# A fused attention and two-MLP kernel: at the passage to the last matrix, landed weight tiles are split before other landed tiles, and the second pass's weights are split five steps later

## The chip, the cores and the metric

The kernel runs on one core of one Trainium2 chip. The core has engines that run side by side, each through its own instructions in program order: TensorE (PE in the rows, its weight loads PEld), VectorE (DVE), ScalarE (ACT), GpSimd (POOL) and SyncE (SP), which here issues every DMA. The metric is device time in microseconds (us), the median over runs of the whole kernel.

## The reference

An attention over 4 x 8 heads of 576 positions (a local part and a part on averaged positions) gives x of 2304 x 512. Two MLPs follow, all in float32:

```python
h = x @ w_in                      # 512 -> 2048
x = (h - tanh(h)) @ w_out         # 2048 -> 512
gate = sigmoid(x @ w_gate)        # 512 -> 1536
val = x @ w_val                   # 512 -> 1536
out = (gate * val) @ w_out2       # 1536 -> 512, the last matrix
```

## The kernel before

**Split operands.** A float32 operand of a large matmul is split into a high part (a rounded copy, made by ACT: "hi") and a low part (operand minus high part, made by DVE: "lo"). One product then is three matmuls in a row on TensorE, `mm3`: L292 (weight high x data high), L293 (weight high x data low) and L294 (weight low x data high). So L292 needs both hi, L293 needs the lo of the data, L294 the lo of the weight.

**The second MLP** is computed in a seven-product scheme for 2 x 2 blocks, so each matrix is stored as seven sums and differences of its blocks (forms). The gate and val stage runs j = 0 to 5 (six pieces of 256 of the 1536 columns), p = 0 to 2 (three pairs of 384-token chunks) and side 0, 1 (gate, val). Its result, gate * val, is made by DVE (L1030), GpSimd forms the sums of it (L1003, in `u_sums`), and SP stores the seven forms of 128 x 384 each to DRAM (names `u_0`, `u_1`, `u_2` for p = 0, 1, 2).

**The last matrix** runs six passes over (p, e): (0,0), (0,1), (1,1), (1,0), (2,0), (2,1); e is one half of the 512 output columns. A pass has six steps i = 0 to 5, a step has seven products in the order `order_b` (forms 0, 4, 3, 5, 1, 2, 6), so a pass is 42 products or 126 matmuls. A weight tile (e, i) holds the seven forms of one step, 128 x 896; (0,0) to (0,5) serve the first pass, (1,0) to (1,5) the second. A data tile (i, form) is one form of step i for one p. The DRAM loads of weight tiles are `w_fetch` (L1057), their hi and lo `w_hi` (L302, through `copy`) and `w_lo` (L1065); of data tiles `u_fetch` (L1080), `u_hi` (L302) and `u_lo` (L1086). In the rows a tile bears the name of the memory that it lies in: weight tiles are `o` or `f` of 128x896, data tiles `x`, `f` or `u` of 128x384 or several of these together. The eight `u` tiles are the last to come in the first pass: form 6 of step 4, and then forms 0 to 6 of step 5.

**What sets the order of the work.** The order on every engine is written out by the program. A counter `now` advances by `tick()`; `defer(n, fn)` puts work n ticks later; "lanes" are generators that are served within ticks under a budget. At the passage from the gate and val stage to the last matrix three lanes run: `first_w` and `first_u` issue the loads as memory comes free, and `first_splits` issues their splits. It takes what was fetched at least six ticks ago, whether the bytes are there or not; the engine that gets the split waits for the bytes:

```python
ready = [x for x in ready if now[0] >= x[0] + 6]
_, kind, x = min(ready)
```

The key of `min` is (tick of the fetch, "u" or "w", tile), so of tiles fetched in one tick the data tiles come first. In the first pass, at the end of step i < 4, the program fetches the second pass's weight tile (1, i+2) 10 ticks later and splits it 10 ticks (hi) and 12 ticks (lo) after that. A step is four ticks. At the end of a pass the seven PSUM banks are read out by ACT (one copy) and DVE (adds, L983), in `out_ends`; later products that use a bank again wait for these.

Of the kernel before, what the change touches and what calls it, by code (L numbers as in the profile page):

```python
# [64 lines left out]
def tile_kernel(ctx: ExitStack, tc: tile.TileContext, qk, vp, v, w1, w2, mask, ident, out):  # L65
# [52 lines left out]
    def defer(n, fn, *args):  # L118
        events.setdefault(now[0] + n, []).append((fn, args))
# [28 lines left out]
    def tick():  # L148
        now[0] += 1
        run_chains(chains.pop(now[0], []))  # L150
        todo = events.get(now[0], [])
        while todo:
            fn, args = todo.pop(0)
            fn(*args)
        events.pop(now[0], None)
        run_later(age=8)
        if beat[0]:
            beat[0]()
        lanes_step()
# [27 lines left out]
    def after(n):  # L187
        at = now[0] + n
        return lambda: now[0] >= at


    loaded, begun, ready, load_at = [0], [0], [0], {}
# [98 lines left out]
    def mm3(o, wh, wl, xh, xl, first, last, **kw):  # L291
        nc.tensor.matmul(out=o, lhsT=wh, rhs=xh, start=first, stop=False, **kw)  # L292
        nc.tensor.matmul(out=o, lhsT=wh, rhs=xl, start=False, stop=False, **kw)  # L293
        nc.tensor.matmul(out=o, lhsT=wl, rhs=xh, start=False, stop=last, **kw)  # L294
# [464 lines left out]
    while any(((1, 0), k) not in xt for k in range(KD)):  # L759
        keep_warm(2)  # L760
        if started[0] < n_first:
            x = items[started[0]]
# [296 lines left out]
    def w_hi(key):  # L1059
        t = w_room[key]  # L1060
        copy(t[:, 0], t[:, 1].bitcast(F32))
# [6 lines left out]
    def pieces(i):  # L1068

        n, todo, at = 7 * i, 7, 0  # L1070
        for g in list(groups):
            size = g[0].shape[1]
            if n < size and todo:
                k = min(size - n, todo)
                yield at, [x[:, n:n + k, :] for x in g]
                at, todo, n = at + k, todo - k, size
            n -= size

    def u_fetch(p, i, at, t):
        nc.sync.dma_start(out=t[1].bitcast(F32), in_=ud[p][:, i, at:at + t[1].shape[1], :])  # L1080

    def u_hi(t):
        copy(t[0], t[1].bitcast(F32))
# [79 lines left out]
    def first_splits():  # L1163

        p = 0
        done = set()
        while len(u_forms) < 7 * NJ or len(fetched_w) < 8 or any(("w", x) not in done for x in fetched_w):
            ready = [(t, "u", x) for x, t in fetched_u.items() if ("u", x) not in done]
            ready += [(t, "w", x) for x, t in fetched_w.items() if ("w", x) not in done]
            ready = [x for x in ready if now[0] >= x[0] + 6]  # L1170
            if not ready:
                yield after(1)
                continue
            _, kind, x = min(ready)
            done.add((kind, x))
            if kind == "w":
                w_hi(x)
                defer(2, w_lo, x)
                yield 1.05
            else:  # L1180
                whole = dict(pieces(x[0]))[x[1]]
                size = whole[0].shape[1]
                for a in range(0, size, 3):
                    t = [y[:, a:min(a + 3, size), :] for y in whole]
                    u_hi(t)
                    defer(2, u_lo, p, x[0], x[1] + a, t)
                    yield 0.1 + 0.45 * t[0].shape[1]

    for j in range(NJ):
        for p in range(len(PAIRS)):  # L1190
            cycle[:] = now[0], p
            for side in range(2):
                while (j, side) not in form or p not in formed:
                    rate[0] = 0.9
                    tick()
                rate[0] = (0.6 if side else 0.9) if j == NJ - 1 else 0.4 if side else 0.65
                w = form[j, side]
                ends = ends_of(j, side, p)
                bank = next(ends)
                if (j, p, side) == (NJ - 1, 0, 0):  # L1200
                    for g in (first_w(), first_u(), first_splits()):
                        lane(g)
                for n, (a, b, at) in enumerate(PRODUCTS):
                    for k in range(2):
                        x = xform[p, k, b]
                        wh, wl = (w[:, i, a, 128 * k:128 * k + 128] for i in range(2))
                        mm3(
                            bank[at], wh, wl, x[:, 0, :], x[:, 1, :], n < 4 and k == 0,
                            k == 1, skip_group_check=n > 3,
                        )  # L1210
                    defer(1, next(ends))
                    tick()
                if p == len(PAIRS) - 1:
                    made.add((j, side))
                made.add((j, side, p))
# [5 lines left out]
    def sum_bank():  # L1221
        n_bank[0] += 1
        k = (n_bank[0] - 1) % 8
        if k < 4:
            return ps.tile([128, 512], F32, tag="ab", bufs=4, name="ab")
        return acc_bank((3, 0, 1, 2)[k - 4])

    def out_ends(q, banks):

        p, e = passes[q]  # L1230
        m1, m6, m5, m7, m2, m3, m4 = (t[:, :N] for t in banks)
        c11, c22, c12, c21 = (xs.tile([128, N], F32, tag="xs", name="c") for _ in range(4))
        to = out[p, e]

        def put(r, half, t, cols=slice(0, N)):
            store(to[:, r, half * N + cols.start:half * N + cols.stop], t[:, cols])

        yield copy(c11, m1)
        yield add(c22, m6, c11)
        yield add(c12, m5, c22)  # L1240
        yield (add(c21, m7, c22), add(c22, m5, c21), defer(1, put, 1, 1, c22))
        yield (add(c11, m2, c11), defer(1, put, 0, 0, c11))
        yield (add(c12, m3, c12), defer(1, put, 0, 1, c12))
        if q < len(passes) - 1:
            yield (add(c21, m4, c21), defer(1, put, 1, 0, c21))
            return
        for cols in (slice(0, N // 2), slice(N // 2, N)):
            add(c21[:, cols], m4[:, cols], c21[:, cols])
            put(1, 0, c21, cols)
        yield None  # L1250

    rate[0] = 0.9
    for q, (p, e) in enumerate(passes):
        ends = None
        for i in range(NJ if q < len(passes) - 1 else NJ - 1):
            both = (i, i + 1) if (q, i) == (len(passes) - 1, NJ - 2) else (i,)
            for m in both:
                while (e, m) not in w_sets or any((p, m, a) not in u_forms for a in range(7)):
                    tick()
            if i == 0:  # L1260
                banks = [sum_bank() for _ in range(7)]
            for n, (a, b) in enumerate(order_b):
                for m in both:
                    x, w = u_forms[p, m, b], w_sets[e, m]
                    mm3(banks[n][:, :N], w[:, 0, a], w[:, 1, a], *x, m == 0, m == NJ - 1)
                if both[-1] == NJ - 1:
                    ends = ends or out_ends(q, banks)
                    defer(1, next, ends)
                if n % 2 or n == 6:
                    tick()  # L1270
            if q + 1 < len(passes) and q % 2 == 0 and i < 4:
                key, wait = (1 - e, (i + 2) % NJ if q == 0 else i), 10 if q == 0 else 1
                defer(wait, w_fetch, key, w_room[e, i])
                defer(wait + 10, w_hi, key)
                defer(wait + 12, w_lo, key)
            if q % 2 and q + 1 < len(passes):
                for k, (at, t) in enumerate(pieces(i)):
                    u_fetch(p + 1, i, at, t)
                    defer(10 + k, u_hi, t)
                    defer(12 + k, u_lo, p + 1, i, at, t)  # L1280
# [70 lines left out]
```

## Time and profile before

| | us |
|---|---|
| median of 3 runs | 923.91 (922.76 to 927.88) |
| the profiled execution: its time | 923.75 |
| the profiled execution: span, first to last instruction | 921.9 |
| TensorE busy | 910.9 (99%) |
| DVE, ACT, POOL busy | 590.1 (64%), 467.1 (51%), 165.1 (18%) |
| first matmul of the last matrix | 785.17 |
| first matmul of its second pass | 808.14 |

The rows below give starts in us from the span's start. A row of a timeline merges neighbours of the same kind: the second number is the time from the first one's start to the last one's end, "x2" the count, and in brackets stands how long the engine sat idle before and what ended that.

### The profile page before, as it was taken

Reading aid. Unit: us, or ns where it says so; the run is one execution under the profiler, and the core shown is the slowest. Engines: PE = TensorE matmul, PEld = TensorE weight load, DVE = VectorE, ACT = ScalarE, POOL = GpSimd, SP = SyncE. Lnnn points to the kernel's source line nnn. Section 1 sums busy time; section 2 is a strip of 40 time slices with the busy share of each in tenths; the row PEclk is TensorE's granted clock in tenths of the full one; section 3 lists DMA queues with packets and bytes.
Section 4 is the critical chain, followed back from the end, with each engine's and each line's share of the span. In section 5 each row is a group of like instructions: output and inputs, shape, how many; then the busy total and the mean of one; then the engine's idle time right before and its main releaser. Section 6 shows DMA issues by size and latency. Waiting matters only on the chain.

```text
span 921.9 us, 16739 instructions
## 1 busy us (share of the span) xinstructions
PE 910.9 (99%) x6392; PEld 876.2 (95%) x6392; DVE 590.1 (64%) x1003; ACT 467.1 (51%) x1166; POOL 165.1 (18%) x185
## 2 busy tenths in 40 slices
PE   7999999999999999999999999999999999999998
PEld 6789989999999999999999999999999999999998
DVE  6799964334343534466875577767767677978582
ACT  5887865444544454443644455353535345655440
POOL 2320102202222020000023243233231314200000
PEclk9999999999999999999999999999999999999999
DMA  8467652222223120457441224343534358987951
GB/s 291 148 233 249 202 156 91 67 62 74 67 66 91 59 78 4 149 217 272 151 141 51 95 95 143 141 168 127 177 115 157 120 161 300 322 294 271 330 203 44
DMA packets 72432, 142.50 MB, mean 155 GB/s; under 512 B 6608, under 2 KB 58400, under 8 KB 68000
## 3 DMA queue, kind: packets, MB, share of 16 engines
q1 hardware_dynamic: 72352, 141.43, 45.3%
q8 instruction: 50, 0.82, 0.4%
q14 instruction: 30, 0.25, 0.1%
HBM read 97.76 MB, written 43.65 MB: 153 GB/s over the span
## 4 chain that ended last, share of the span: by engine, by line
PE 86%; issue 5%; DVE 2%; ACT 2%; DMA 2%; POOL 1%; SPq 0%; POOLq 0%; DVEq 0%
PE ab L292 13%; PE acc L292 13%; PE ab L294 13%; PE ab L293 13%; PE acc L293 13%; PE acc L294 12%; PE ab L539 2%; PE ab L457 1%; PE ab L530 1%; PE acc L755 1%; PE ab L426 1%; PE ab L374 1%; DMA u<-t 1%; PE ab L408 1%; POOL t L1003 1%
## 5 line engine op out<-in xcount | busy, mean ns | idle before, releaser
L305 DVE TENSOR_TENSOR t<-ab,t 128x384 f32<-128x384 f32 x94 | 52.3, 556 | 136.0 <-ACT t L657 135.6
L292 PE MATMUL acc<-g,w 128*128 128x384 f32 x384 | 132.6, 347 | 0.0
L292 PE MATMUL ab<-x,w 128*128 128x384 f32 x376 | 130.8, 348 | 0.1
L293 PE MATMUL acc<-g,w 128*128 128x384 f32 x384 | 129.5, 337 | 0.0
L294 PE MATMUL acc<-g,w 128*128 128x384 f32 x384 | 129.4, 337 | 0.0
L294 PE MATMUL ab<-x,w 128*128 128x384 f32 x376 | 126.5, 336 | 0.0
L293 PE MATMUL ab<-x,w 128*128 128x384 f32 x376 | 126.4, 336 | 0.0
L657 ACT ACTIVATE t<-ab 128x384 f32<-128x384 f32 x94 | 45.9, 488 | 131.0 <-PE ab L294 128.8
L294 PE MATMUL ab<-x,f 128*128 128x384 f32 x261 | 87.8, 336 | 0.8 <-DVE f L1065 0.8
L294 PE MATMUL acc<-x,f 128*128 128x384 f32 x261 | 87.6, 336 | 0.0
L292 PE MATMUL acc<-x,f 128*128 128x384 f32 x261 | 87.6, 336 | 0.0
L293 PE MATMUL acc<-x,f 128*128 128x384 f32 x261 | 87.6, 336 | 0.0
L293 PE MATMUL ab<-x,f 128*128 128x384 f32 x261 | 87.6, 336 | 0.0
L292 PE MATMUL ab<-x,f 128*128 128x384 f32 x261 | 87.6, 336 | 0.0
L305 DVE TENSOR_TENSOR g<-t,g 128x384 fp32r<-128x384 f32 x96 | 56.0, 584 | 39.8 <-ACT g L302 38.5
L292 PEld LDWEIGHTS acc<-g,w 128*128 128x128 f32 x384 | 72.1, 188 | 2.2 <-issue 1.2
L292 PEld LDWEIGHTS ab<-x,w 128*128 128x128 f32 x376 | 70.7, 188 | 3.1 <-issue 1.4
L293 PEld LDWEIGHTS acc<-g,w 128*128 128x128 f32 x384 | 72.3, 188 | 0.4 <-issue 0.2
L294 PEld LDWEIGHTS acc<-g,w 128*128 128x128 f32 x384 | 72.2, 188 | 0.1
L302 ACT ACTIVATE g<-t 128x384 fp32r<-128x384 f32 x96 | 50.0, 522 | 42.1 <-DVE t L305 42.0
L293 PEld LDWEIGHTS ab<-x,w 128*128 128x128 f32 x376 | 70.8, 188 | 0.1
L294 PEld LDWEIGHTS ab<-x,w 128*128 128x128 f32 x376 | 70.7, 188 | 0.1
(186 smaller groups left out, 2018.7 us busy)
## 6 DMA issues: line engine op xcount, KB each, us to landing
raw<-in_w SPq DMA_DIRECT2D x34, 1024.0 KB
u<-t SPq DMA_DIRECT2D x51, 192.0 KB
qk<-in_qk SPq DMA_DIRECT2D x16, 576.0 KB
x<-u SPq DMA_DIRECT2D x9, 960.0 KB
o<-o SPq DMA_DIRECT2D x18, 448.0 KB
u<-c SPq DMA_DIRECT2D x39, 192.0 KB
u<-c SPq DMA_DIRECT2D x18, 384.0 KB
o<-f SPq DMA_DIRECT2D x6, 896.0 KB
```

Of the source, the lines that this page charges most:

```text
L292: nc.tensor.matmul(out=o, lhsT=wh, rhs=xh, start=first, stop=False, **kw)
L293: nc.tensor.matmul(out=o, lhsT=wh, rhs=xl, start=False, stop=False, **kw)
L294: nc.tensor.matmul(out=o, lhsT=wl, rhs=xh, start=False, stop=last, **kw)
L302: nc.scalar.activation(out=dst, in_=src, func=ACTF.Copy)
L305: nc.vector.tensor_tensor(out=dst, in0=a, in1=b, op=ALU.subtract)
L374: nc.tensor.matmul(out=sd[t][o0:o0 + 64, at, :], lhsT=qd[r0:r0 + 64, 40 * j:40 * j + 64], rhs=kd[r0:r0 + 64, :], start=True, stop=True,)
L408: nc.tensor.transpose(out=tb[:, 128 * j:128 * j + 128], in_=pd[:, j, 72 * f:72 * f + 72], identity=id_sb)
L426: nc.tensor.matmul(out=ob[64 * h:64 * h + 64, :], lhsT=vd[:, f, 64 * h:64 * h + 64], rhs=pdt[:, f, h].rearrange("p j k -> p (j k)"), start ...
L457: nc.tensor.matmul(out=bank[o0:o0 + 64, at, :], lhsT=t[r0:r0 + 64, 0, QB * j:QB * j + QB], rhs=t[r0:r0 + 64, 1, w0:w0 + WIN], start=True, ...
L530: nc.tensor.transpose(out=tb[:, j, :], in_=pl[:, 3 * f + j, :], identity=id_sb)
L539: nc.tensor.matmul(out=ob[r0:r0 + 64, QB * x:QB * x + QB], lhsT=vw[0][:, j - n, i, r0:r0 + 64], rhs=pt[:, x, o0:o0 + 64], start=True, stop ...
L657: nc.scalar.activation(out=t, in_=hb[:, :N], func=ACTF.Tanh)
```

## The change

`first_splits` takes weight tiles before data tiles, whatever the tick of their fetch; the lo of such a weight tile is put one tick after its hi, not two; and in the first pass hi and lo of the second pass's weight tiles come 15 and 17 ticks after the fetch, not 10 and 12. The fetches themselves are as before.

```diff
-            _, kind, x = min(ready)
+            _, kind, x = min(ready, key=lambda y: (y[1] != "w", y[0], y[2]))
             done.add((kind, x))
             if kind == "w":
                 w_hi(x)
-                defer(2, w_lo, x)
+                defer(1, w_lo, x)
                 yield 1.05
...
                 key, wait = (1 - e, (i + 2) % NJ if q == 0 else i), 10 if q == 0 else 1
+                gone = 15 if q == 0 else 10
                 defer(wait, w_fetch, key, w_room[e, i])
-                defer(wait + 10, w_hi, key)
-                defer(wait + 12, w_lo, key)
+                defer(wait + gone, w_hi, key)
+                defer(wait + gone + 2, w_lo, key)
```

What this does to the order of instructions is shown at three places. The first is ACT at the end of the first pass, before the change. The `f` 128x896 are the weight tiles (0,4) and (0,5), the `u` the last eight data tiles of the first pass, the first two `o` behind them (1,0) and (1,1), `c<-ab` is the first read-out of the first pass's banks, the next four `o` are (1,2) to (1,5), and the `x` are data tiles of the third pass:

```order
L302 ACTIVATE f<-f 128x896 x2
L302 ACTIVATE u<-u 128x384 x8
L302 ACTIVATE o<-o 128x896 x2
L302 ACTIVATE c<-ab 128x384
L302 ACTIVATE o<-o 128x896 x4
L302 ACTIVATE x<-x 128x5x384
L302 ACTIVATE x<-x 128x2x384
L302 ACTIVATE x<-x 128x3x384
```

And after the change:

```order
L302 ACTIVATE f<-f 128x896 x2
L302 ACTIVATE o<-o 128x896 x2
L302 ACTIVATE u<-u 128x384 x8
L302 ACTIVATE c<-ab 128x384
L302 ACTIVATE o<-o 128x896 x3
L302 ACTIVATE x<-x 128x5x384
L302 ACTIVATE x<-x 128x2x384
L302 ACTIVATE o<-o 128x896
L302 ACTIVATE x<-x 128x3x384
```

The two `o` of the second pass, (1,0) and (1,1), moved in front of the eight `u` of the first pass; (1,5) moved behind seven data tiles of the third pass; (1,2), (1,3) and (1,4) kept their place.

The second place is DVE at the same point, with the lo parts, before the change:

```order
L1065 TENSOR_TENSOR f<-f 128x896 x2
L1086 TENSOR_TENSOR u<-u 128x384 x8
L1065 TENSOR_TENSOR o<-o 128x896 x2
L983 TENSOR_TENSOR c<-ab,c 128x384 x4
L983 TENSOR_TENSOR c<-acc,c 128x384 x3
L1065 TENSOR_TENSOR o<-o 128x896 x4
```

And after it:

```order
L1065 TENSOR_TENSOR f<-f 128x896 x2
L1065 TENSOR_TENSOR o<-o 128x896 x2
L1086 TENSOR_TENSOR u<-u 128x384 x8
L983 TENSOR_TENSOR c<-ab,c 128x384 x4
L983 TENSOR_TENSOR c<-acc,c 128x384 x3
L1065 TENSOR_TENSOR o<-o 128x896 x3
```

Here too the lo parts of (1,0) and (1,1) moved in front of those of the eight `u`, and the read-out of the banks (L983) now follows the `u` and no longer the `o`.

The third place is DVE some 15 us earlier, around the last two products gate * val (L1030, the second of which GpSimd's last sums need), before the change. The `o` here are the weight tiles (0,2) and (0,3):

```order
L983 TENSOR_TENSOR c<-acc,three 128x384
L1086 TENSOR_TENSOR x<-x 128x2x384
L1030 TENSOR_TENSOR c<-c 128x768
L983 TENSOR_TENSOR c<-acc,three 128x384
L1086 TENSOR_TENSOR x<-x 128x384
L1030 TENSOR_TENSOR c<-c 128x768
L1086 TENSOR_TENSOR x<-x 128x2x384
L1065 TENSOR_TENSOR o<-o 128x896 x2
```

And after it:

```order
L983 TENSOR_TENSOR c<-acc,three 128x384
L1086 TENSOR_TENSOR x<-x 128x384
L1030 TENSOR_TENSOR c<-c 128x768
L983 TENSOR_TENSOR c<-acc,three 128x384
L1086 TENSOR_TENSOR x<-x 128x3x384
L1030 TENSOR_TENSOR c<-c 128x768
L1086 TENSOR_TENSOR x<-x 128x2x384
L1086 TENSOR_TENSOR x<-x 128x384
```

The `o` of (0,2) and (0,3) moved some ten instructions forward, in front of all these rows, so each data tile here stands later, and between the two L1030 there is now one of three tiles where there was one of one. On TensorE nothing moved; on SP the fetch of (1,5) moved in front of the fourth store of the first pass's output.

## Rows read from the trace of the kernel before

**Rows 1.** The page: span, and busy time of each engine.
```profile
span 921.9 us, 16739 instructions
...
PE 910.9 (99%) x6392; PEld 876.2 (95%) x6392; DVE 590.1 (64%) x1003; ACT 467.1 (51%) x1166; POOL 165.1 (18%) x185
```

**Rows 2.** Windows, the first three passes: length, busy per engine (count), clock, DMA.
```profile
785.17:808.14 22.97, 22.15 (x127) 21.83 (x127) 22.30 (x28) 15.12 (x23) 6.27 (x4) 1.00 0.94 325
808.14:830.50 22.36, 22.03 (x126) 21.50 (x126) 15.67 (x20) 11.32 (x12) 0.00 (x0) 1.00 0.83 289
830.50:852.70 22.20, 22.20 (x130) 22.20 (x129) 18.49 (x27) 13.05 (x19) 0.00 (x0) 1.00 0.78 269
```

**Rows 3.** Waits of TensorE from 600 us on: total, times, longest.
```profile
PE ab L294 <- DVE f L1065: 0.8, 1, 0.8
PE ab L292 <- DVE c L983: 0.3, 1, 0.3
```

**Rows 4.** Timeline of TensorE, end of the first pass, start of the second.
```profile
799.90 0.34 PE L293 MATMUL ab<-x,f 128*128 128x384 f32 x1
801.05 0.44 PE L294 MATMUL ab<-x,f 128*128 128x384 f32 x1 [0.82 <-DVE f L1065]
...
803.93 0.33 PE L292 MATMUL acc<-u,f 128*128 128x384 f32 x1
...
805.15 0.34 PE L293 MATMUL ab<-u,f 128*128 128x384 f32 x1
...
809.58 0.34 PE L294 MATMUL ab<-x,o 128*128 128x384 f32 x1
810.25 0.44 PE L292 MATMUL ab<-x,o 128*128 128x384 f32 x1 [0.33 <-DVE c L983]
```

**Rows 5.** Timeline of ACT, the same stretch and the second pass.
```profile
801.45 1.99 ACT L302 ACTIVATE u<-u 128x384 fp32r<-128x384 f32 x4 [0.46 <-DMA u<-u]
...
805.37 0.95 ACT L302 ACTIVATE o<-o 128x896 fp32r<-128x896 f32 x1 [0.61 <-DMA o<-o]
806.52 0.96 ACT L302 ACTIVATE o<-o 128x896 fp32r<-128x896 f32 x1 [0.19 <-DMA o<-o]
...
820.74 3.81 ACT L302 ACTIVATE x<-x 128x1920 fp32r<-128x1920 f32 x3 [1.65 <-DMA x<-u]
```

**Rows 6.** Timeline of DVE, last gate products to second pass.
```profile
787.83 1.13 DVE L1086 TENSOR_TENSOR x<-x 128x384 fp32r<-128x384 f32 x1
788.89 0.94 DVE L1030 TENSOR_TENSOR c<-c 128x768 f32<-128x768 f32 x1
...
790.62 3.73 DVE L1065 TENSOR_TENSOR o<-o 128x896 fp32r<-128x896 f32 x2
...
801.92 3.83 DVE L1086 TENSOR_TENSOR u<-u 128x384 fp32r<-128x384 f32 x8
806.36 2.24 DVE L1065 TENSOR_TENSOR o<-o 128x896 fp32r<-128x896 f32 x2 [0.61 <-ACT o L302]
808.52 2.27 DVE L983 TENSOR_TENSOR c<-ab,c 128x384 f32<-128x384 f32 x4
...
822.58 6.19 DVE L1086 TENSOR_TENSOR x<-x 128x1920 fp32r<-128x1920 f32 x4 [2.36 <-ACT x L302]
```

**Rows 7.** Timeline of POOL, sums of the last product gate * val.
```profile
787.53 1.02 POOL L1003 TENSOR_TENSOR t<-c 128x384 f32<-128x384 f32 x1 [9.05 <-DVE c L1030]
...
793.49 1.75 POOL L1003 TENSOR_TENSOR c<-c,t 128x384 f32<-128x384 f32 x1
```

**Rows 8.** Timeline of SP: last store of sums, first fetches of the next weights.
```profile
795.26 0.32 SPq L309 DMA_DIRECT2D u<-c  x1
...
799.71 3.02 SPq L1057 DMA_DIRECT2D o<-o  x5
```

**Rows 9.** Line 755 on TensorE, 0 to 9 us and 12 to 20 us: ns min/median/max.
```profile
L755 PE MATMUL acc<-id_sb x10: 421/421/581, 4.8 to 8.8; 128*128 128x128 f32 x10
...
L755 PE MATMUL acc<-id_sb x42: 275/275/377, 12.2 to 19.7; 128*128 128x128 f32 x42
```

## The prediction

> **What bounds the kernel now.** I read the page first: TensorE is busy 910.9 of 921.9 us, the next engine, DVE, 64% [rows 1]. So any time that TensorE is made to wait is added to the span, and a saving on another engine is worth only the wait that it takes away. The next view is therefore the list of TensorE's waits in the part that the change touches. There are two, of 0.8 and 0.3 us [rows 3]. The timeline gives their full cost as the gap between starts, less the 0.17 us at which matmuls follow each other (22.20 us for 126 to 130 of them in an undisturbed pass [rows 2]). The first is 801.05 - 799.90 - 0.17 = 0.98 us: L294 of tile (0,4) waits for DVE's lo of that weight tile. The second is 810.25 - 809.58 - 0.17 = 0.50 us: the fourth product of the second pass waits for a bank that DVE has yet to read out [rows 4]. Together 1.5 us; the third pass shows none [rows 2]. More than 1.5 us can hardly be won here, 0.16% of the whole.
>
> The timelines of ACT and DVE then show how near the passage runs to a wait elsewhere. The last eight data tiles of the first pass have their hi on ACT from 799 on; a run of four took 1.99 us, so the pitch is 0.49. Their lo run on DVE from 801.92, eight in 3.83 us, a pitch of 0.47 with 0.55 for one [rows 5, 6]. TensorE takes the first of them, form 6 of step 4, at 803.93. The one that comes closest is form 4 of step 5: sixth of the eight in DVE's order, but third in the order of use. Its lo ends at 801.92 + 5 x 0.47 + 0.55 = 804.82, and TensorE reads it at 805.15 [rows 4]. That is 0.33 us of slack. Right behind the eight come the hi of (1,0) and (1,1), and both had to wait for their bytes: they start at 805.37 and 806.52, each released by its DMA [rows 5]. SP issued these transfers from 799.71 on [rows 8], so the first took 5.7 us.
>
> **The change, part by part.**
>
> *The pair (1,0), (1,1) in front of the eight data tiles.* This is the large term. "Landed" in the program means fetched six ticks ago, and on the chip these two have not landed when ACT reaches them. ACT works in order, so it now stands before (1,0) until 805.37, ends (1,1) at 806.52 + 0.96 = 807.48, and only then begins the hi of the eight tiles, the first of which had long been there. DVE does the lo of the pair as before, 806.36 + 2.24 = 808.60, and starts the eight at about 808.52 (starts overlap ends by some 0.1 us in these rows; the row of L983 that stands there now shows it [rows 6]). The sixth lo ends at 808.52 + 5 x 0.47 + 0.55 = 811.42. ACT is no slower: the sixth hi ends at about 807.4 + 5 x 0.49 + 0.52 = 810.4. TensorE reads form 4 of step 5 at 811.47 where it did at 805.15: 6.3 us later. A matmul that waited also takes 0.1 us longer (0.44 against 0.34 [rows 4]), so +6.4. The products around it do not add: form 6 of step 4 has its lo at 809.07 and is done long before 811.4, and those behind it find a lo every 0.47 us while TensorE needs 0.53 for a product.
>
> *The wait of 0.98 us* sits ahead of this one. If it went, TensorE would only reach form 6 of step 4 earlier and wait longer. It is worth nothing in the sum. I doubt that it goes at all: the lo of (0,2) and (0,3) still stand in front of (0,4) on DVE, only further ahead, and DVE was busy without a gap up to there.
>
> *The wait of 0.50 us* goes. The read-out by DVE stood behind the lo of the pair; now it stands behind the eight lo, which end at 808.52 + 7 x 0.47 + 0.55 = 812.4, while TensorE ends the first pass at about 814.6 (811.76 for L294 of the late product, then five products of 0.53). The read-out keeps up with the products: -0.5.
>
> *(0,2) and (0,3) further forward.* Their two lo no longer run from 790.62, where they took 3.73 us against 2.24 for a like pair later [rows 6]; GpSimd was at its sums then [rows 7]. So two-input work on DVE is slower while GpSimd works, and what stands there instead pays that. It matters at one place: between the two L1030 there is now a tile of three in place of a single one. The single one took 1.13 us beside GpSimd's 1.02, against 0.47 to 0.55 elsewhere [rows 6, 7]. A tile of three costs 3 x 0.47 = 1.4 us alone, and 2.0 with the same 0.6 on top, so the second L1030 moves by 0.3 to 0.9 us, less about 0.1 that DVE is ahead at the first. GpSimd's sums hang on it, their last store leaves SP at 795.26, as the last sum ends (793.49 + 1.75), and all fetches of the eight tiles and of the pair are queued behind this store on SP [rows 7, 8]. So the whole of the large term moves by 0.2 to 0.8 us. I take 0.7, since the row beside GpSimd is the nearer one. The lower bound of the term is -0.1, if the order up to there gives back more than it costs.
>
> *Splits of the second pass five steps later.* Tiles (1,2), (1,3), (1,4) stand at the same place on ACT and DVE as before, as nothing else was queued in those steps: no cost, no gain. Only (1,5) falls behind seven data tiles of the third pass. Its cover is the time until step 5 of the second pass: the pass began at 808.14, and its last 21 matmuls start 3.7 us before its end at 830.50, at 826.8 [rows 2]. If those seven land as late after the start of the pass as they did (820.74, [rows 5]), DVE ends them at 822.58 + 6.19 x 7/14 = 825.7 and the lo of (1,5) at 826.8; L294 needs it at 827.1. So nothing, with a slack of 0.3. I expect more, since SP's issue of those loads waits for TensorE alone once the read-outs come early. If that slack is gone it costs up to 0.7.
>
> **The sum**, against the profiled execution's own 923.75 us (0.16 below the median of the three runs): 923.75 + 6.4 - 0.5 + 0.7 = 930.35, say 930.3. Later passes give nothing back, since TensorE has no further wait that could shrink [rows 2, 3].
>
> **The rivals.**
>
> *The clock falls in the stall.* TensorE will stand still from about 804 to 808.6 and then work in bits until 812. The granted clock is 1.00 (2.4 GHz) in all passes [rows 2], and no row of this trace has such a stall behind a busy stretch. The nearest thing is the start: after the engine had been idle for 4.8 us, line 755's matmuls took 421 ns until 8.8 us and 275 ns later [rows 9], 4.0 us of slow work. Were that to come again at about half the pace, 2.0 us would be lost: 932.4. The Trainium skill ("TensorE: Matmul & The Clock Gate", section "Why this matters for your kernels") warns that idle gaps between bursts of matmuls send the clock back to half rate, and by it this rival would be the forecast. I give it 0.20: only the first piece of the idle time is long, and unlike the start it comes after hundreds of us of dense work.
>
> *(1,5) comes late as well*: a wait of 0.7 at step 5 of the second pass, 931.0. For it speaks the slack of 0.3, against it the earlier issue. 0.07.
>
> *Not slower.* If the bytes of (1,1) were there 6.3 us earlier, by 800.2, ACT would not wait, the eight lo would come in time, and the 0.98 and 0.50 us would be won: 922.3. It decides at 0.5 us after the issue at 799.71, where the trace shows 5.7 for the first of the two; SP's order does not move there. 0.04.
>
> *A smaller stall*: the pair lands 1 to 3 us earlier since transfers around it move, 927.5 to 929.3. The DMA engines are 94% busy in this pass [rows 2], so little is to be had. 0.07.
>
> **How the numbers follow.** The forecast has 0.62, with its own range of 929.5 to 931.3 (-0.1 to 0.8 in place of 0.7, and some tenths between executions). What a measurement of this kernel can tell from no change is about 0.5%, 4.6 us: 928.5 is the bound. Above it lie the forecast, the clock's rival, the late (1,5) and a part of the smaller stall: slower 0.88, same 0.11, faster 0.01. The range takes in the clock's rival and part of the smaller stall: 928.2 to 932.9, leaving out some 0.15.
>
> **What would show it.** In the trace after: TensorE waits once for ACT's hi of a `u` tile for over 4 us near 804 to 809, and then for DVE's lo of a `u` for about 1 us twice; ACT idles from 796 until the DMA of `o` releases it near 806, then does `o` twice and `u` eight times without a gap; the wait L292 on DVE's L983 is gone; the second pass starts near 815.3; the later passes last 22.2 to 22.4 us. If the matmuls behind the stall follow at more than 0.17 us, the clock's rival holds. The prediction is wrong if the pair's DMA lands before 802, or if ACT takes the `u` tiles first.

## The result and the profile after

The changed kernel takes 931.79 us (median of six runs, 930.24 to 933.38); the kernel before took 924.39 us beside it (six runs, 922.76 to 927.88). The ratio is 1.0076 with an interval of 1.0054 to 1.0097: slower by 7.0 us, between 5.0 and 9.0 (the two medians lie 7.4 apart). The forecast of 930.3 was 1.5 us short. The time lies in its range, but just outside the likeliest case's own range (up to 931.3) and beside the rival in which the clock falls (932.4).

The profiled execution took 932.47 us. Its page, span and busy time of each engine, to be read against [rows 1]:

```profile
span 930.7 us, 16743 instructions
...
PE 914.9 (98%) x6392; PEld 879.4 (94%) x6392; DVE 590.7 (63%) x1003; ACT 465.4 (50%) x1166; POOL 164.9 (18%) x185
```

The span grew by 8.8 us. TensorE's busy time grew by 4.0 with the same 6392 matmuls, so not all of the loss is idle time. The waits of TensorE from 780 us on (total, times, longest), against [rows 3]:

```profile
PE acc L292 <- ACT u L302: 4.5, 1, 4.5
PE ab L294 <- DVE f L1065: 0.8, 1, 0.8
PE acc L293 <- DVE u L1086: 0.6, 1, 0.6
```

The wait of 0.8 on the lo of (0,4) is still there. The wait on the bank read-out (L983) is gone, and two waits for the eight `u` data tiles are new. The timeline of TensorE shows where they lie (start, length, then the idle time in front and who ended it), against [rows 4]:

```profile
804.59 0.34 PE L294 MATMUL acc<-x,f 128*128 128x384 f32 x1
809.46 0.59 PE L292 MATMUL acc<-u,f 128*128 128x384 f32 x1 [4.54 <-ACT u L302]
810.64 0.69 PE L293 MATMUL acc<-u,f 128*128 128x384 f32 x1 [0.59 <-DVE u L1086]
811.13 0.52 PE L294 MATMUL acc<-u,f 128*128 128x384 f32 x1
811.45 0.52 PE L292 MATMUL ab<-u,f 128*128 128x384 f32 x1
...
812.41 0.52 PE L292 MATMUL ab<-u,f 128*128 128x384 f32 x1
812.99 0.69 PE L293 MATMUL ab<-u,f 128*128 128x384 f32 x1
...
816.35 0.38 PE L294 MATMUL acc<-u,f 128*128 128x384 f32 x1
816.57 0.34 PE L292 MATMUL acc<-u,f 128*128 128x384 f32 x1
...
817.62 0.34 PE L292 MATMUL acc<-x,o 128*128 128x384 f32 x1
```

L294 at 804.59 is the last matmul for which there is data. Behind the stall the matmuls follow each other at 0.32 us (811.13 to 811.45), where [rows 4] and the rest of the trace have 0.17; only from 816.57 on is it 0.17 again. The matmul at 812.99 is L293 on form 4 of step 5; the second pass begins at 817.62. The windows of the same stretch (length, busy time of PE, PEld, DVE, ACT, POOL, then granted clock, DMA share, GB/s) say why:

```profile
785.98:804.80 18.82, 17.99 (x103) 17.47 (x102) 16.85 (x18) 8.03 (x12) 5.61 (x4) 1.00 0.91 309
804.80:809.46 4.66, 0.13 (x1) 0.00 (x0) 1.52 (x2) 2.36 (x4) 0.00 (x0) 1.00 0.97 371
809.46:816.40 6.94, 6.29 (x18) 5.39 (x19) 5.97 (x12) 5.86 (x11) 0.00 (x0) 0.51 0.03 12
816.40:817.60 1.20, 1.20 (x8) 1.20 (x7) 1.17 (x4) 0.00 (x0) 0.00 (x0) 0.99 0.00 0
```

The granted clock was 1.00 (2.4 GHz) up to the stall, 0.51 (1.2 GHz) for the 6.9 us behind it, then 0.99 again. This was so not in the profiled run alone: each of the six runs has a mean granted clock of 0.996, where the fast runs of the kernel before have 0.999 or 1.000.

The second pass itself is now free of waits. It began at 808.14 before and at 817.62 after; the third pass begins at the first of these rows before, and at the second after:

```profile
830.76 0.34 PE L292 MATMUL acc<-x,o 128*128 128x384 f32 x1
839.51 0.34 PE L292 MATMUL acc<-x,o 128*128 128x384 f32 x1
```

So the second pass takes 21.89 us, and took 22.62 (the window of [rows 2] that ends at 830.50 stops 0.26 short of its end). ACT's timeline, against [rows 5], gives the cause of the stall:

```profile
796.26 0.96 ACT L302 ACTIVATE f<-f 128x896 fp32r<-128x896 f32 x1 [2.04 <-DMA f<-o]
806.92 0.95 ACT L302 ACTIVATE o<-o 128x896 fp32r<-128x896 f32 x1 [9.70 <-DMA o<-o]
808.05 0.95 ACT L302 ACTIVATE o<-o 128x896 fp32r<-128x896 f32 x1 [0.18 <-DMA o<-o]
808.90 3.40 ACT L302 ACTIVATE u<-u 128x384 fp32r<-128x384 f32 x8
```

ACT stands for 9.70 us before the first tile of the pair, until its DMA lands, and does the eight `u` without a gap behind it. DVE, against [rows 6], makes the second L1030 at 790.38, and later waits for ACT's hi of the pair:

```profile
790.38 0.94 DVE L1030 TENSOR_TENSOR c<-c 128x768 f32<-128x768 f32 x1
...
807.90 2.22 DVE L1065 TENSOR_TENSOR o<-o 128x896 fp32r<-128x896 f32 x2 [5.07 <-ACT o L302]
810.04 3.83 DVE L1086 TENSOR_TENSOR u<-u 128x384 fp32r<-128x384 f32 x8
814.10 0.56 DVE L983 TENSOR_TENSOR c<-ab,c 128x384 f32<-128x384 f32 x1 [0.23 <-PE ab L294]
```

The last matrix begins 0.81 us later in this trace than before (785.98 against 785.17 in [rows 2]), in a part that the change leaves alone; kernels that are identical up to there began it anywhere from 785.17 to 787.01. So traces are compared here by their *stage*: from the first matmul of the last matrix to the end of the span. It is 921.9 - 785.17 = 136.73 us before and 930.7 - 785.98 = 144.72 after, 7.99 more.

### The profile page after: what moved, and what is told of

The parts are those of the page before. It is cut to its first block, busy times and chain, and to the rows that moved or that the text cites. A ratio compares the mean times of both kernels' runs of the same rounds, so it can differ in the third digit from the quotient of the medians.

```text
span 930.7 us, 16743 instructions
## 1 busy us (share of the span) xinstructions
PE 914.9 (98%) x6392; PEld 879.4 (94%) x6392; DVE 590.7 (63%) x1003; ACT 465.4 (50%) x1166; POOL 164.9 (18%) x185
## 4 chain that ended last, share of the span: by engine, by line
PE 88%; issue 5%; DMA 2%; ACT 1%; DVE 1%; POOL 1%; SPq 0%; POOLq 0%; DVEq 0%
PE ab L292 13%; PE acc L292 13%; PE ab L293 13%; PE ab L294 13%; PE acc L293 13%; PE acc L294 13%; PE ab L539 2%; PE ab L530 2%; PE ab L457 1%; PE ab L374 1%; PE acc L755 1%; PE ab L426 1%; PE ab L408 1%; DMA u<-t 1%; POOL t L1003 1%
## 5 line engine op out<-in xcount | busy, mean ns | idle before, releaser
L293 PE MATMUL acc<-g,w 128*128 128x384 f32 x384 | 129.5, 337 | 0.0
L294 PE MATMUL acc<-g,w 128*128 128x384 f32 x384 | 129.4, 337 | 0.0
L293 PE MATMUL ab<-x,w 128*128 128x384 f32 x376 | 126.5, 336 | 0.0
L294 PE MATMUL ab<-x,w 128*128 128x384 f32 x376 | 126.5, 336 | 0.0
L294 PE MATMUL ab<-x,f 128*128 128x384 f32 x261 | 87.8, 336 | 0.8 <-DVE f L1065 0.8
L294 PE MATMUL acc<-x,f 128*128 128x384 f32 x261 | 87.7, 336 | 0.0
L293 PE MATMUL acc<-x,f 128*128 128x384 f32 x261 | 87.6, 336 | 0.0
L293 PE MATMUL ab<-x,f 128*128 128x384 f32 x261 | 87.6, 336 | 0.0
L293 PEld LDWEIGHTS acc<-g,w 128*128 128x128 f32 x384 | 72.3, 188 | 0.4 <-issue 0.2
L294 PEld LDWEIGHTS acc<-g,w 128*128 128x128 f32 x384 | 72.2, 188 | 0.1
L293 PEld LDWEIGHTS ab<-x,w 128*128 128x128 f32 x376 | 70.8, 188 | 0.1
L294 PEld LDWEIGHTS ab<-x,w 128*128 128x128 f32 x376 | 70.7, 188 | 0.1
```

## The experiments

All times in the table are worked out from the profiles: us since the first matmul of the last matrix. "Pair" is the start of the hi of (1,0), "u" that of the first of the eight data tiles, both on ACT, "second pass" its first matmul on TensorE. The ratio is to the kernel before, with its interval. The kernel before, run beside each group of experiments, had medians of 924.76 to 925.49 us; expectations that give a time for the whole kernel count from a kernel before of about 924.4 and lie up to 1 us low for that.

| kernel | pair | u | second pass | stage | ratio |
|---|---|---|---|---|---|
| before | 20.20 | 13.92 | 22.97 | 136.73 | |
| after | 20.94 | 22.92 | 31.64 | 144.72 | 1.0076 [1.0054, 1.0097] |
| steps alone | 20.29 | 13.26 | 23.00 | 136.79 | 1.0004 [0.9994, 1.0014] |
| weights first alone | 20.74 | 22.73 | 31.40 | 144.51 | 1.0085 [1.0069, 1.0101] |
| pair behind | 21.17 | 12.95 | 24.24 | 138.07 | 1.0009 [0.9997, 1.0021] |
| pair behind, lo as before | 20.82 | 13.00 | 22.99 | 137.46 | 1.0007 [0.9998, 1.0016] |
| pair fetched early | 9.79 | 14.74 | 24.81 | 137.90 | 1.0008 [0.9999, 1.0017] |
| before, pair fetched early | 20.65 | 16.28 | 23.21 | 137.03 | 0.9990 [0.9980, 1.0001] |
| one tile in front | 20.63 | 21.48 | 31.08 | 144.12 | 1.0071 [1.0053, 1.0089] |
| TensorE kept busy, 20 | 21.20 | 23.23 | 30.41 | 143.52 | 1.0069 [1.0054, 1.0085] |
| TensorE kept busy, 40 | 20.41 | 22.35 | 31.93 | 145.02 | 1.0091 [1.0076, 1.0106] |
| before, (1,1) later | 20.04 | 13.54 | 22.99 | 136.09 | 1.0001 [0.9992, 1.0009] |
| after, gate product early | 20.07 | 22.05 | 29.83 | 142.89 | 1.0080 [1.0063, 1.0096] |
| before, gate product late | 21.62 | 13.21 | 23.11 | 138.16 | 0.9997 [0.9988, 1.0006] |

**Which half of the change.** First the five steps alone, with the choice in `first_splits` as before:

```diff
+                gone = 15 if q == 0 else 10
-                defer(wait + 10, w_hi, key)
-                defer(wait + 12, w_lo, key)
+                defer(wait + gone, w_hi, key)
+                defer(wait + gone + 2, w_lo, key)
```

> Only the second part of the change: hi and lo of the second pass's weight tiles 15 and 17 ticks after the fetch, the choice in the passage as before. My theory (all of the loss comes from the pair (1,0), (1,1) standing in front of the eight data tiles): no change, 924.4 us within 0.7, and the lo of (1,5) still ends before TensorE needs it. Rival (the later splits make the second pass wait): a wait of TensorE on a weight tile of the second pass, and 926 us or more.

It took 925.71 us, beside 925.46 for the kernel before, and its stage is that of before within 0.06. Then the other half, the changed kernel with the steps back at 10 and 12:

```diff
-                gone = 15 if q == 0 else 10
+                gone = 10
```

> The first half of the change alone: landed weight tiles are split before landed data tiles, and the splits of the second pass's weights stay 10 and 12 ticks behind their fetch. My theory: all of the loss comes from this half, so the ratio to the kernel before is 1.0076 (1.005 to 1.010), TensorE waits some 4.5 us for ACT's hi of a `u`, the granted clock falls behind it, and from the first matmul of the last matrix to the end of the span it takes 144.7 us (before 136.73, with the whole change 144.72). Rival, the five steps carry a part of the loss (they set when (1,5) is split and what stands ahead of the third pass's data): the stage would be 143.5 or less.

It took 932.46 us. The stage is 144.51, TensorE waits 4.3 us for ACT, and behind that the matmuls follow at 0.32 us again. So the whole loss comes from the order of the splits.

**Which tiles.** The changed kernel with only the first pass's weights, (0,2) to (0,5), ahead of data; the second pass's pair behind:

```diff
-            _, kind, x = min(ready, key=lambda y: (y[1] != "w", y[0], y[2]))
+            _, kind, x = min(ready, key=lambda y: (y[1] != "w" or y[2][0] == 1, *y))
```

> The changed kernel, but weight tiles go first only if they are of the first pass; (1,0) and (1,1) stand behind the data tiles again, (0,2) and (0,3) stay forward. My theory: nearly all of the loss goes, 924.4 to 925.3 us; the upper end if the sums on GpSimd, and with them the fetch of the eight data tiles, still come 0.7 us later than before. Rival (moving (0,2) and (0,3) is a large part of the loss): 927 us or more.

The loss is gone but for 1.3 us of the stage. The waits of TensorE in this kernel name the rest:

```profile
PE acc L293 <- DVE u L1086: 1.0, 1, 1.0
PE ab L294 <- DVE f L1065: 0.8, 1, 0.8
PE ab L292 <- DVE c L983: 0.3, 1, 0.3
```

One of its ten runs took 931.37 us with a mean granted clock of 0.996, as in the changed kernel; that run has no trace, and why the clock fell in it stays open.

The new wait is the 1.0 on a `u`. The change also puts the lo one tick after the hi, and with that the lo of (1,0) still stood on DVE in front of the last `u`. So this was not a clean test; one with two ticks for the pair was:

```diff
-                defer(1, w_lo, x)
+                defer(2 if x[0] else 1, w_lo, x)
```

> The changed kernel with hi and lo of (1,0) and (1,1) both behind the eight data tiles (in the earlier try the lo of (1,0) still stood in front of the last of them); (0,2) and (0,3) and the later splits of the second pass stay as changed. My theory: only the later sums of GpSimd are left, 0.7 us less the 0.3 of slack: 137.2 us for the last matrix (136.8 before), 0.4 us more in the median. Rival (moving (0,2) and (0,3) costs more): 138.1 or more, as in the earlier try.

The second pass now starts at 22.99, as before (22.97): the pair in front of the eight `u` is the cause, and the first pass's own weights further forward cost TensorE nothing. Its stage of 137.46 is 0.7 above that of before because the pair landed 0.62 later, and the wait for the read-out behind it came twice.

**Whether the bytes are what ACT waits for.** The changed kernel with the same order on ACT and DVE, but with the loads of the pair issued in front of those of the eight `u`, 13.4 us earlier:

```diff
-            (lambda: (5, 6) in fetched_u, "b", 6),
+            (lambda: (4, 1) in fetched_u, "b", 6),
```

> The changed kernel with the same order on every compute engine; only the loads of (1,0) and (1,1) are issued right behind those of (0,4) and (0,5), some 13 us earlier on the queue. My theory (the loss is ACT's wait for bytes, not the work of the two tiles): ACT does the pair in its idle stretch before the data tiles, the wait of over 4 us goes, and only DVE's two lo, 2.2 us, stand in the way: 924.5 to 927 us, 925.4 as the likeliest, and no fall of the clock. Rival (the work in front is the cost, or the queue only gives the delay to the data tiles): 929 us or more.

ACT's timeline in this kernel:

```profile
796.59 0.96 ACT L302 ACTIVATE o<-o 128x896 fp32r<-128x896 f32 x1 [0.16 <-DMA o<-o]
797.74 0.95 ACT L302 ACTIVATE o<-o 128x896 fp32r<-128x896 f32 x1 [0.19 <-DMA o<-o]
801.54 1.67 ACT L302 ACTIVATE u<-u 128x384 fp32r<-128x384 f32 x3 [2.85 <-DMA u<-u]
```

The pair is split in the time in which ACT waits for bytes anyway, the stall of 4.5 us does not occur, and the ratio falls from 1.0076 to 1.0008. So it was ACT's wait for the bytes that made the order dear. What is left, 1.2 us of the stage, is on DVE, as the expectation had it. Its timeline:

```profile
803.57 2.08 DVE L1065 TENSOR_TENSOR o<-o 128x896 fp32r<-128x896 f32 x2
805.57 3.83 DVE L1086 TENSOR_TENSOR u<-u 128x384 fp32r<-128x384 f32 x8
```

The lo of the pair still stand in front of the eight `u`, and DVE works here without a gap. Its sixth lo ends at 805.57 + 5 x 0.47 + 0.55 = 808.47, which is 21.67 us after the first matmul of the last matrix, and TensorE reads that tile at 808.51; in the kernel before the sixth lo ends at 19.65. The eight `u` also land later, behind the pair's 917 KB (two tiles of 128 x 896 in float32): their first hi starts at 14.74, where in kernels with the pair behind it is at 12.95 to 13.92. But the hi of the sixth ends at 805.06, 2.9 us before DVE comes to it, so this later landing costs nothing here.

The same early fetch in the kernel before, with the pair last in the choice, could be a gain if the wait of 0.50 us went:

```diff
-            (lambda: (5, 6) in fetched_u, "b", 6),
+            (lambda: (4, 1) in fetched_u, "b", 6),
...
-            _, kind, x = min(ready)
+            _, kind, x = min(ready, key=lambda y: (y[1] == "w" and y[2][0] == 1, *y))
```

> The kernel before, its order kept on every compute engine, with the loads of (1,0) and (1,1) issued 13 us earlier, behind those of (0,4) and (0,5). My theory: ACT does the pair right behind the data tiles without waiting for bytes, the read-out of the banks comes earlier, and the wait of 0.5 us at the start of the second pass goes: 136.3 us for the last matrix against 136.8, too little for the median to show. Rival: the earlier loads push back the eight data tiles and TensorE waits for them: 137.5 or more.

A miss. The eight `u` now land late (16.28), ACT and DVE reach the pair no earlier than before (20.65), and the wait for the bank stays. The ratio's interval touches 1.

**Half of the pair.** The changed kernel with only (1,0) in front; the code is that of the kernel with the pair behind and the lo as before, with `y[2] == (1, 1)` and `x == (1, 1)` in the two conditions.

> The changed kernel, but of the pair only (1,0) stands in front of the eight data tiles, (1,1) behind them. My theory: ACT is released by the first of the two transfers, 1.1 us earlier, and DVE has one lo less in front; the sixth data tile's lo ends 1.15 us earlier. From the first matmul of the last matrix to the end of the span (136.8 us before, 144.7 after) that gives 143.6 us if the clock falls again and about 142.1 if the shorter idle stretch of 3.7 us leaves it at 1.00. Rival (the number of tiles in front does not matter): 144.7.

One tile is nearly as dear as two: 7.4 us of the stage against 8.0. The wait gets shorter by 1.4 us, but the clock falls all the same. Rows of TensorE's timeline in this kernel:

```profile
804.88 0.34 PE L294 MATMUL acc<-x,f 128*128 128x384 f32 x1
808.32 0.44 PE L292 MATMUL acc<-u,f 128*128 128x384 f32 x1 [3.10 <-ACT u L302]
809.51 0.44 PE L293 MATMUL acc<-u,f 128*128 128x384 f32 x1 [0.74 <-DVE u L1086]
...
810.13 0.34 PE L293 MATMUL ab<-u,f 128*128 128x384 f32 x1
810.30 0.43 PE L294 MATMUL ab<-u,f 128*128 128x384 f32 x1
810.53 0.55 PE L292 MATMUL ab<-u,f 128*128 128x384 f32 x1
811.85 0.69 PE L293 MATMUL ab<-u,f 128*128 128x384 f32 x1 [0.77 <-DVE u L1086]
```

After the long wait of 3.10 us the matmuls still follow at 0.17; the slow pace begins only at about 810.4, when TensorE was working again in bits. From form 4 of step 5 (811.85) to the second pass (817.36) it takes 5.51 us, where it is 4.63 in the changed kernel and 2.99 in the kernel before: the slow stretch began later, more of it lies behind that product, and this takes back most of what the shorter wait gave.

**What the clock takes.** The changed kernel with matmuls of the identity matrix, whose result nothing reads, in the place of the stall. With 40 of them TensorE was busy for 8.9 us, longer than the stall (a matmul of this kind shows as two rows, x80, and takes 0.22 us):

```diff
+                if (q, i, n) == (0, 4, 6):
+                    warm = acc_bank(2)
+                    for _ in range(40):
+                        nc.tensor.matmul(out=warm[:, :128], lhsT=id_sb, rhs=id_sb, start=True, stop=True)
```

> The changed kernel with 40 matmuls of 128x128 on the identity matrix (into a bank that is free then, the result unused) just in front of the product that waits, so that TensorE works through the long wait. The theory that the clock fell because of the idle wait: the long wait shrinks to under 1 us, the granted clock stays at 1.00, the matmuls behind it follow every 0.17 us instead of 0.32, and the second pass starts about 1.5 us earlier: 930.3 us. Rival (the matmuls there are slow for another reason, such as data arriving late): they stay at 0.32 and the time at 931.8 us.

This was sized wrongly: the clock stayed at 1.0, but the filling itself ended over 4 us after the first `u` was split. So the same with 20:

> The changed kernel with 20 matmuls on the identity in front of the product that waits; 40 took 8.9 us, twice the length of the wait, so 20 should take 4.5 and end as the data tile arrives. If the fall of the clock costs the 1.5 us that I read from the trace, the granted clock stays at 1.00 and the last matrix takes 143.2 us from its first matmul to the end of the span, not 144.7. Rival: the clock costs nothing of its own since TensorE would wait for DVE's lo anyway: 144.7.

TensorE's timeline in that kernel:

```profile
804.96 4.63 PE L1266 MATMUL acc<-id_sb 128*128 128x128 f32 x40
809.97 0.44 PE L292 MATMUL acc<-u,f 128*128 128x384 f32 x1 [0.38 <-ACT u L302]
811.15 0.44 PE L293 MATMUL acc<-u,f 128*128 128x384 f32 x1 [0.74 <-DVE u L1086]
...
812.12 0.35 PE L292 MATMUL ab<-u,f 128*128 128x384 f32 x1
813.49 0.44 PE L293 MATMUL ab<-u,f 128*128 128x384 f32 x1 [1.01 <-DVE u L1086]
...
816.59 0.34 PE L292 MATMUL acc<-x,o 128*128 128x384 f32 x1
```

Windows of the filled stretch and of the one behind it:

```profile
804.96:809.50 4.54, 4.54 (x41) 4.43 (x40) 1.09 (x1) 1.90 (x3) 0.00 (x0) 1.00 0.96 351
809.97:816.59 6.62, 4.87 (x25) 4.28 (x25) 6.48 (x14) 5.74 (x11) 0.00 (x0) 1.00 0.08 30
```

The clock stays at 1.00, though behind the filling TensorE waits twice for DVE and is busy for only 4.87 of 6.62 us; so it was the long idle wait that made it fall. From L293 on form 4 of step 5 to the second pass it is 816.59 - 813.49 = 3.10 us here, 808.14 - 805.15 = 2.99 in the kernel before [rows 2, 4], and 817.62 - 812.99 = 4.63 in the changed kernel. So the fallen clock takes 1.5 us. The stage gains only 1.2 of it, since the pair landed 0.26 later than in the changed kernel; the intervals of the two ratios overlap.

**The bank wait by itself.** The kernel before, with the splits of (1,1) alone four ticks later, so that DVE reads out six of the seven banks before the lo of (1,1):

```diff
-                w_hi(x)
-                defer(2, w_lo, x)
+                late = 4 if x == (1, 1) else 0
+                if late:
+                    defer(late, w_hi, x)
+                else:
+                    w_hi(x)
+                defer(late + 2, w_lo, x)
```

> The kernel before, but the hi and lo of the single weight tile (1,1) go 4 ticks later in the passage, so that DVE reads out all but one of the first pass's banks before the lo of (1,1). My theory: the wait of 0.50 us for a bank at the start of the second pass is due to the lo of the pair standing in front of the read-out; it goes, nothing else changes, and the stage from the first matmul of the last matrix to the end of the span takes 136.2 us (before 136.73); the ratio is 0.9995, which five rounds can hardly tell from 1. Rival: (1,1) is then late for step 1 of the second pass, 3.7 us after its start, and TensorE waits there for its lo: 137 us or more.

The wait for L983 is gone, (1,1) is not waited for, and the stage is the shortest of all, 136.09, 0.64 below before. The median of 924.73, beside 924.76 for the kernel before, does not tell the two apart: a gain of 0.07% of the time lies below what such runs show.

**What moves the landing of the pair.** Of the twelve traces up to here, seven have the new order of (0,2) and (0,3) and load the pair last; its hi starts at 20.41 to 21.20 in them. In the three with the old order it starts at 20.04 to 20.29. Two kernels were to tell an effect of the second L1030 from mere scatter. The changed kernel, with the lo of the tile of three (the eighth that `first_splits` takes) behind that L1030:

```diff
-                    defer(2, u_lo, p, x[0], x[1] + a, t)
+                    cnt[0] += 1
+                    defer(3 if cnt[0] == 8 else 2, u_lo, p, x[0], x[1] + a, t)
```

> The changed kernel with one edit: the lo of the tile of three that stands between the last two L1030 on DVE goes behind the second of them. What is open: in all seven traces with the changed order of (0,2) and (0,3) the hi of (1,0) starts 20.41 to 21.20 us after the first matmul of the last matrix, in the three with the old order at 20.04 to 20.29, while GpSimd's last sum and the issue of the loads stand still. Theory one: the second L1030 moves it (0.68 later with the change), through the stores that follow it. Here that L1030 comes about 1.9 us earlier than in the changed kernel, so the pair lands at 20.3 or before, and the second pass starts near 31.0 (31.64 with the change). Theory two: it is the scatter of the transfers, or the place of the (0,2) and (0,3) splits: the pair stays at 20.4 to 21.2. The ratio is 1.007 by either.

And the kernel before with the same edit for the ninth tile:

> The kernel before with one edit: the lo of a tile of two goes behind the first of the last two L1030 on DVE, so that the second comes about 1.4 us later than before (at some 5.1 us after the first matmul of the last matrix, before 3.72). Theory one, that this L1030 moves the landing of the pair: its hi starts at 20.9 or later. Theory two, scatter or the place of the (0,2) and (0,3) splits: it starts at 20.0 to 20.3 as in the three traces with the old order, unless GpSimd's last sum itself ends later and takes the issue of the loads with it, which the rows of POOL and SP would show (last sum at 10.08, issue of the pair's load at 14.5). The ratio is 1.000 to 1.001 by either.

In the first the L1030 came at 2.65 and the pair at 20.07, as the theory of the L1030 has it; but GpSimd's last sum ended early as well, at 9.19, and SP issued the load of the pair at 13.96. POOL's row and ACT's:

```profile
794.59 1.21 POOL L1003 TENSOR_TENSOR c<-c,t 128x384 f32<-128x384 f32 x1
```

```profile
806.68 0.95 ACT L302 ACTIVATE o<-o 128x896 fp32r<-128x896 f32 x1 [10.63 <-DMA o<-o]
```

In the second the edit did not do what I wanted: the first L1030 came earlier, and the second only 0.14 later (3.86). Yet this kernel, with the old order, has the latest pair of all, at 21.62. ACT's row:

```profile
809.16 0.95 ACT L302 ACTIVATE o<-o 128x896 fp32r<-128x896 f32 x1 [2.21 <-DMA o<-o]
```

SP's issue of its load came at 15.21, and from there it took 6.4 us; over all traces with this order of loads it was 13.96 to 15.44 and then 5.4 to 6.4. So the landing scatters by more than the 0.74 us between the two profiled executions, whatever the order of the splits. The first of the two kernels also shows the clock in another length: granted 0.51 for 3.4 us only, and 3.69 us from form 4 of step 5 to the second pass.

```profile
810.60:814.00 3.40, 3.13 (x10) 2.62 (x10) 3.17 (x8) 3.27 (x7) 0.00 (x0) 0.51 0.01 2
```

This short stretch is that of the profiled run (931.29 us, mean granted clock 0.998). The other three runs have 0.996, as the changed kernel, and took 931.61 to 933.12 us; so the ratio of 1.0080 is no smaller, though the stage of the one trace is.

## Why the prediction was right, and where it was not

**The pair in front of the eight tiles, +6.4: right.** ACT waited for the bytes of (1,0) until 806.92, did the pair and then the eight `u` in one run, as said; with the bytes early the stall is gone, and with the pair behind as well. DVE's sixth lo ends at 810.04 + 5 x 0.47 + 0.55 = 812.94, and TensorE reads form 4 of step 5 at 812.99. Since the start of the last matrix that is 27.01 us, before it was 19.98: 7.03 later, 6.3 of which are this term and 0.74 the later landing of the pair. Of the two waits for a lo of DVE that were forecast, one shows (0.6 us); at the other, form 4 of step 5, matmuls at half the pace filled most of the time.

**GpSimd's last sums later, +0.7: the size came, the step was wrong.** The second L1030 did move by 0.68 (4.40 after the start of the last matrix, 3.72 before). But the sums did not follow it. POOL's timeline after, against [rows 7]:

```profile
791.40 1.67 POOL L1003 TENSOR_TENSOR t<-c 128x384 f32<-128x384 f32 x1 [2.16 <-DVE c L1030]
793.04 1.33 POOL L1003 TENSOR_TENSOR t<-c,t 128x384 f32<-128x384 f32 x1
794.45 1.62 POOL L1003 TENSOR_TENSOR c<-c,t 128x384 f32<-128x384 f32 x1
```

They began 0.67 later and ended at 10.09 us after the start of the last matrix, before at 10.07: two of the three were shorter (the last 1.62 against 1.75). In all traces but the two of the last experiments this end lies between 10.06 and 10.10, and in the trace after SP issued the load of the pair at 14.54, as before. Why the sums end at the same time in both orders was not tried. For the chain from L1030 over the sums to the pair speaks one trace, the kernel with the gate product early: the sums ended 0.90 earlier than in the changed kernel, the load was issued 0.58 and the pair came 0.87 earlier. But the issue scatters from 14.54 to 15.44 over traces whose sums end alike, so the chain is not shown. What made the pair 0.74 later here (20.94 against 20.20) lies between issue and landing, 6.40 us against 5.66, and the last experiment finds as much without the change. Whether a part of the 0.74 belongs to the change stays open.

**The clock, rival at 0.20: came true on top of the forecast.** This is the step that failed in the likeliest case. The argument against it was that only the first piece of the idle time is long, and that it comes after hundreds of us of dense work. Neither helped: the rows show 0.51 directly behind a wait of 4.5 us, and in the kernel with one tile in front 0.50 after 3.1 us and some work in bits. By the rule of the Trainium skill that was cited ("TensorE: Matmul & The Clock Gate", section "Why this matters for your kernels") this rival would have been the forecast, and the windows agree with it. Its price was 2.0 us, half of 4.0 us of slow work at the start [rows 9]; in the trace after it measured 1.5. That these two lie so near is luck in part: the slow stretch was 6.9 us long, but in its first half, up to 812.99, TensorE had DVE's lo to wait for anyway. With it the sum is 930.35 + 1.5 = 931.85, against a median of 931.79. This agreement too is closer than the terms behind it: the sum starts from the 923.75 of one execution, and the kernel before took 924.39 in the median beside the changed one. In the stage, where that does not enter, it is 6.6 + 1.5 = 8.1 against 7.99. Over the kernels the price varied: the one with the gate product early had 0.51 for half as long in its trace, and lost 3.69 - 3.10 = 0.6; the one with one tile in front, whose slow stretch began later, lost 5.51 - 3.10 = 2.4.

**The wait of 0.50 us gone, -0.5: right, and a little more.** From the start of the second pass to the end of the span it is 113.08 us after and 113.76 before, 0.68 less, and the kernel with (1,1) later finds the same alone (113.10). All of it is in the second pass, 22.62 us before and 21.89 after. Beside the wait of 0.50, three matmuls of that pass started 0.04 to 0.11 late before the change, too little to stand in the list of waits; these are gone as well.

**The wait of 0.98 us: stayed**, as doubted; every kernel that was run shows it, with 0.8 or 0.9 us of idle time. **Splits five steps later: nothing**, as said. The lo of (1,5) ends at 832.91 after, and step 5 of the second pass begins 21 matmuls before 839.51, at 835.8: 3 us to spare, where the sum had left 0.3. (The sum took 830.50, the end of a window, for the end of the pass, which is 830.76; by its own working the slack was nearer 0.6.)

In all: 7.03 at form 4 of step 5, 4.63 - 2.99 = 1.64 for the clock (with some 0.1 for a matmul that waited longer), less 0.68, are the 7.99 of the stage. One sum of chances was slightly off: 0.62, 0.20 and 0.07 make 0.89 already, so 0.88 was too little for slower.

## What to carry to other kernels

"Issued some ticks ago" is not "landed": before a step is moved forward on an engine that works in order, look up in the trace when its DMA releases it, and count what then queues behind it. If TensorE is made to stand for some microseconds, put the slow matmuls behind the stall into the sum; hundreds of us of dense work before it did not help here. And where a landing scatters by 1 us from trace to trace, a term of 0.7 us can come out right for the wrong reason.

## What the runs showed of the hardware

The granted clock fell to 0.51 after 4.5 us of idle time amid dense work, and was back after 6.9 us of work at the slow pace; after a like wait of 3.7 us in the kernel with the gate product early it was back after 3.4 us. It did not always fall at once: behind the wait of 3.1 us six matmuls ran at full pace, and then 6.7 us at the slow one followed, though TensorE was at work for most of them. In one kernel with a wait of 1.0 us in its trace, one of ten runs had a mean granted clock of 0.996, which no trace explains. Twenty matmuls that nobody reads, 4.5 us of work, held the clock at 1.00 through the stall, but bought back only what the slow pace had cost.

Two-input work on GpSimd and DVE took longer at places where they ran side by side: DVE's lo of three tiles took 1.94 us in the trace after, with GpSimd at work, and 1.36 in the trace before, with GpSimd idle; GpSimd's last three sums took 1.33 to 1.87 us each in the two traces, where it took 1.0 with DVE idle. Yet these sums ended within 0.03 us of each other over two orders of DVE's work, though the last two took 1.33 and 1.62 us in the one and 1.87 and 1.75 in the other.
